# Attention and two MLPs on one core: when weights are loaded and converted beside attention, and which engine casts the activations

## The chip, the cores and the metric

The kernel runs on one core of a Trainium2 chip. The metric is the device time of one execution in microseconds (us). The runs of the kernel before took 685.08, 686.46 and 688.02 us, median 686.46. The execution that the profiler recorded took 685.12 us, of which the trace covers a span of 683.3 us; the remaining 1.8 us lie before the first and after the last recorded instruction. Differences of about half a per cent, some 3.4 us, are the smallest that can be told from no change here.

## What is computed

The reference, cut to what matters:

```python
def attention(q, k, v, n_global=8, n_local=96):      # batch 2, heads 8, seq 768, head_dim 64, fp32
    scores = q @ k.T / 8 - slope[h] * dist            # dist from |i-j|, or n_local for global columns
    keep = (j < n_global) | (0 <= i - j < n_local)
    a = softmax(where(keep, scores, -1e9))
    return a @ v

x = attention(...)            # laid out as 1536 tokens x 512
h = x @ w_in                  # 512 x 2048
g = max(h, 0) + log1p(exp(-abs(h)))
x = g @ w_out                 # 2048 x 512
h = x @ w_in2
out = (h * clip(h + 3, 0, 6) / 6) @ w_out2
```

The weights arrive as 8-byte floats. The kernel reads them as pairs of 32-bit words and makes two fp32 parts of each number, a high and a low one. Activations are split in the same way. Each product of the MLPs is then three matmuls: low by high, high by low, high by high.

## The kernel before, in words

**Tiles.** A chunk is 128 of the 2048 hidden columns of a layer; there are 16 per layer. One chunk's `w_in` is a unit, and its `w_out` another, each 512 KB in HBM and 128x512 numbers in SBUF. The class `Layers` keeps six slots for finished chunks beside attention (`FIRST_SLOTS`) and gets five more (`MORE_SLOTS`) when attention's memory is given back (`grow`).

**The order of units.** `self.order` (lines 68 to 70) puts first the `w_in` units of chunks 0 to 5 (units 0 to 5 here), then the `w_out` units of chunks 0 to 5 (units 6 to 11), then chunk by chunk. `unit_load` (L102 to L107) asks SP for the 512 KB into a tile `raw`. `unit_convert` (L109 to L134) makes the two parts in seven steps on three engines: absolute value on ScalarE (L121), clamp on GpSimd (L124), shift (L125) and two merges with the raw words (L128, L129) on VectorE, the cast of the high part (`cast`, L98 on GpSimd while `in_first` holds, L100 on ScalarE afterwards) and the subtraction that gives the low part on VectorE (L134). Each step needs the one before it. The low part is what TensorE waits for.

**Raw buffers.** There are two `raw` and two `wa` tiles beside attention (pool `wr0`), and two more of each after `grow`. `weight_step` (L136 to L147) keeps loads ahead of the conversions by as many units as there are raw buffers.

**The first part of the program.** It mixes attention with the first phase of layer 0, which runs over chunks 0 to 5 in pairs. Attention is cut into 24 quads (four heads of 128 rows); a quad has a score step `s` (TensorE scores L445, VectorE bias and row minimum L451, ScalarE exponential L456, row sums L341 and L342 on VectorE, normalisation of `pm` on GpSimd L344), two transpose steps `t` (L477, copied by ScalarE L479) and a value step `v` (L495; the result is cast at L502 and split at L503). Five quads are started ahead of the first matmul of the MLP, in the loop with `LEAD_UNITS`, the number of units that `weight_step` converts after each of the five.

`run` then goes over halves of items. An item is 256 tokens with one pair of chunks; its first half (`first_h`, tile `hf`) makes `h`, then `split_g` makes `g` and its two parts (`ghf`, `glf`), and its second half (`first_o`, tile `accf`) multiplies by `w_out`. The halves come as h0, h1, h2, o0, h3, o1, h4, o2, h5, o3 and so on. Each half carries one score step and one value step ahead of its 24 matmuls, and transposes after the sixth and the eighteenth. After the matmuls of a half it calls `weight_step` with the next number of `HALF_UNITS` (L313 and L314). So before, units 0 to 3 are asked for in the lead, unit 4 after h0, unit 5 after h1, units 6 and 7 after h2, and one more after each of o0, h3, o1 and h4. h2 needs units 4 and 5, o0 needs 6 and 7, o1 needs 8 and 9, o2 needs 10 and 11.

**What sets the order.** A scheduler places the instructions of each engine. Instructions given to `keep_in_program_order` keep their order among themselves: TensorE's in this part, and L121. Everything else goes where the scheduler's own estimate puts it, after what it depends on. On the chip each engine then takes its list strictly in that order, so that one instruction that waits holds all behind it.

**Between the parts.** After 20 halves all quads are done; `run` closes attention's pools and calls `grow`. The rest of the first phase (h11, o9 and so on to o17) runs without attention, together with the conversion of units 12 to 21. Then follow the phases of whole items (`item`), 512 tokens and one chunk each.

Of the kernel before, what the change touches and what calls it, by code (L numbers as in the profile page):

```python
# [10 lines left out]
I32 = mybir.dt.int32  # L11
# [5 lines left out]
P = 128  # L17
# [8 lines left out]
CW = 512  # L26
# [4 lines left out]
LEAD_UNITS = (0, 1, 1, 1, 1)  # L31
HALF_UNITS = (1, 1, 2, 1, 1, 1, 1)
# [16 lines left out]
class Layers:  # L49
# [6 lines left out]
    def __init__(self, ctx, tc, weights, xsh, xsl, out):  # L56
        self.ctx, self.tc, self.nc = ctx, tc, tc.nc
        self.weights, self.xsh, self.xsl, self.out = weights, xsh, xsl, out
        self.pool("mp", 2)
        self.pool("tp", 5)  # L60
        self.pool("pp", 1)
        self.part = [self.pp.tile([P, 4, GB], F32, name=f"part{g}") for g in range(T // GB)]
        self.three = self.pp.tile([P, 1], F32, name="three")
        self.nc.vector.memset(self.three, 3.0)
        self.W, self.raws, self.slot = {}, {}, {}
        self.done, self.loaded = 0, 0
        first = range(PHASES[0][0])
        self.order = [(j, u) for u in range(2) for j in first]
        self.order += [(j, u) for j in range(len(first), 2 * NCH) for u in range(2)]
        self.free, self.h_tags, self.acc_tags, self.wr = [], [], [], []  # L70
        self.n_h, self.halves, self.in_first = 0, 0, True
        self.grow(0, FIRST_SLOTS, 2, 2)
# [22 lines left out]
    def cast(self, out, in_):  # L95

        if self.in_first:
            self.nc.gpsimd.tensor_scalar(out=out, in0=in_, scalar1=1.0, scalar2=0.0, op0=ALU.mult, op1=ALU.add)  # L98
        else:
            self.nc.scalar.copy(out, in_)  # L100

    def unit_load(self, x):  # L102
        j, u = self.order[x]
        layer, f = divmod(j, NCH)
        raw = self.wr[x % len(self.wr)].tile([P, CW, 2], I32, tag="raw", name=f"raw{j}_{u}")
# [30 lines left out]
    def weight_step(self, m):  # L136
        total = 4 * NCH
        for _ in range(m):
# [3 lines left out]
            while self.loaded <= min(x + 2 * len(self.wr) - 1, total - 1):  # L142
                self.unit_load(self.loaded)
                self.loaded += 1
# [3 lines left out]
    def split_g(self, layer, hf, n):  # L148
# [6 lines left out]
        if layer == 0:  # L155
# [3 lines left out]
            if self.in_first:  # L159
# [10 lines left out]
        self.cast(gh, t3)  # L170
# [114 lines left out]
    def run(self, att=None, spare_step=lambda: None):  # L285
# [20 lines left out]
        for i in range(n):  # L306
            if not grown and (att is None or att.done()):
                if att:
                    att.close()
                self.grow(1, MORE_SLOTS, 2, 2)  # L310
# [36 lines left out]
def fast_path(tc, ident, nf, q, k, qt, kt, v, weights, out, flag):  # L347


    with ExitStack() as ctx, ExitStack() as actx:  # L350
        nc = tc.nc
        xsh, xsl = x_tiles(ctx, tc)
        layers = Layers(ctx, tc, weights, xsh, xsl, out)
        tp = layers.tp
        ap2 = actx.enter_context(tc.tile_pool(name="ap2", bufs=2))
# [410 lines left out]
```

## Time and profile before

| | |
|---|---|
| runs, us | 685.08, 686.46, 688.02 |
| profiled execution, us | 685.12 (span 683.3) |
| TensorE busy | 634.4 us, 93% of the span |
| VectorE busy | 437.8 us, 64% |
| ScalarE busy | 357.2 us, 52% |
| GpSimd busy | 166.4 us, 24% |
| mean granted TensorE clock | 0.972 of full speed |
| HBM traffic | 53 MB, 77 GB/s over the span |

PE is TensorE's matmul stream and PEld its weight loads, DVE is VectorE, ACT is ScalarE, POOL is GpSimd, SP the engine that issues all DMAs. Busy shares of TensorE also count time at half clock, so the share alone does not tell the work that is done. The page cuts the span into 40 slices of 17.1 us; a digit is the busy share in tenths. Views of the trace give, for a wait, the engine and line that ended it ("<-").

### The profile page before, as it was taken

Reading aid. Unit: us, or ns where it says so; the run is one execution under the profiler, and the core shown is the slowest. Engines: PE = TensorE matmul, PEld = TensorE weight load, DVE = VectorE, ACT = ScalarE, POOL = GpSimd, SP = SyncE. Lnnn points to the kernel's source line nnn. Section 1 sums busy time; section 2 is a strip of 40 time slices with the busy share of each in tenths; the row PEclk is TensorE's granted clock in tenths of the full one; section 3 lists DMA queues with packets and bytes.
Section 4 is the critical chain, followed back from the end, with each engine's and each line's share of the span. In section 5 each row is a group of like instructions: output and inputs, shape, how many; then the busy total and the mean of one; then the engine's idle time right before and its main releaser. Section 6 shows DMA issues by size and latency. Waiting matters only on the chain.

```text
span 683.3 us, 9612 instructions
## 1 busy us (share of the span) xinstructions
PE 634.4 (93%) x3481; PEld 522.1 (76%) x3481; DVE 437.8 (64%) x894; ACT 357.2 (52%) x749; POOL 166.4 (24%) x237
## 2 busy tenths in 40 slices
PE   8764876999997999999999999999999999999996
PEld 4553766888996988787888888888888788888884
DVE  6868345555399999999998999322752424324243
ACT  6945434776553477677677765233667222222221
POOL 4884433433255442234320021000100000000000
PEclk9988888999999999999999999999999999999998
DMA  7433323121023224142320123100265000001011
GB/s 231 143 113 116 109 66 116 39 67 55 33 93 124 94 92 147 70 154 93 123 94 31 62 64 121 63 0 1 78 197 157 1 1 0 1 0 62 0 63 66
DMA packets 24936, 53.66 MB, mean 79 GB/s; under 512 B 2480, under 2 KB 8880, under 8 KB 24880
## 3 DMA queue, kind: packets, MB, share of 16 engines
q1 hardware_dynamic: 24880, 52.96, 23.9%
q8 instruction: 29, 0.48, 0.3%
q14 instruction: 27, 0.22, 0.1%
HBM read 49.81 MB, written 3.15 MB: 77 GB/s over the span
## 4 chain that ended last, share of the span: by engine, by line
PE 65%; DVE 21%; ACT 5%; POOL 3%; issue 3%; DMA 1%; POOLq 0%; DVEq 0%; SPq 0%; ACTq 0%
PE acc L179 27%; PE h L179 26%; PE hf L179 4%; DVE wa L128 4%; PE accf L179 3%; DVE w L134 3%; DVE wa L129 3%; ACT pm L456 2%; POOL pm L344 2%; PE ptp L477 2%; PE s L445 2%; DVE wa L125 2%; PE px L495 1%; DVE pm L451 1%; DVE t2f L164 1%
## 5 line engine op out<-in xcount | busy, mean ns | idle before, releaser
L179 PE MATMUL h<-xsh,w 128*128 128x512 f32 x624 | 170.5, 396 | 1.9 <-DVE t3f L165 1.6
L179 PEld LDWEIGHTS h<-xsh,w 128*128 128x128 f32 x624 | 116.7, 188 | 30.6 <-DVE t3f L165 1.8
L179 PE MATMUL acc<-w,gh 128*128 128x512 f32 x384 | 120.6, 395 | 0.0
L124 POOL TENSOR_SCALAR wa<-wa 128x512 f32<-128x512 f32 x64 | 66.4, 1041 | 219.5 <-ACT wa L121 218.0
L169 DVE SCALAR_TENSOR_TENSOR t<-t,h 128x512 f32<-128x512 f32 x48 | 32.9, 686 | 98.2 <-ACT t L168 98.1
L168 ACT ACTIVATE t<-h,three 128x512 f32<-128x512 f32 x48 | 33.0, 687 | 107.2 <-PE h L179 107.0
L179 PE MATMUL h<-xsl,w 128*128 128x512 f32 x312 | 86.7, 395 | 0.0
L179 PE MATMUL accf<-ghf,w 128*128 128x256 f32 x288 | 66.8, 312 | 20.5 <-DVE w L134 20.4
L179 PEld LDWEIGHTS acc<-w,gh 128*128 128x128 f32 x384 | 72.0, 188 | 17.5
L171 DVE TENSOR_TENSOR gl<-t,gh 128x512 fp32r<-128x512 f32 x78 | 55.4, 710 | 46.3 <-ACT gh L100 46.1
L179 PE MATMUL acc<-gh,w 128*128 128x512 f32 x240 | 78.2, 396 | 1.3 <-DVE part L264 1.3
L100 ACT CAST gh<-t 128x512 fp32r<-128x512 f32 x78 | 48.3, 619 | 58.2 <-PE acc L179 25.6
L179 PE MATMUL acc<-w,gl 128*128 128x512 f32 x192 | 76.1, 396 | 0.1
L179 PEld LDWEIGHTS accf<-ghf,w 128*128 128x128 f32 x288 | 52.5, 211 | 23.2 <-DVE w L134 21.7
L179 PEld LDWEIGHTS h<-xsl,w 128*128 128x128 f32 x312 | 58.5, 188 | 14.0
L344 POOL TENSOR_SCALAR pm<-pm,rs 128x256 f32<-128x256 f32 (+1 forms) x96 | 52.5, 565 | 46.9 <-DVE rs L342 35.1
L134 DVE TENSOR_TENSOR w<-wa,w 128x512 fp32r<-128x512 f32 x64 | 46.5, 730 | 16.2 <-POOL w L98 8.9
L179 PEld LDWEIGHTS acc<-gh,w 128*128 128x128 f32 x240 | 45.1, 188 | 12.9 <-ACT t L157 1.7
L121 ACT ACTIVATE wa<-raw 128x512 f32<-128x512 f32 x64 | 42.5, 673 | 22.8 <-DVE w L134 14.4
L456 ACT ACTIVATE pm<-pm,nm 128x256 f32<-128x256 f32 (+1 forms) x96 | 46.2, 484 | 14.8 <-DVE nm L451 14.7
L179 PE MATMUL hf<-xsh,w 128*128 128x256 f32 x288 | 45.7, 290 | 7.9 <-DVE w L134 7.9
L451 DVE CUSTOM_DVE_ANT_0 pm<-s,bias 128x256 f32<-128x256 f32 (+1 forms) x96 | 33.4, 397 | 28.9 <-PE s L445 27.2
(90 smaller groups left out, 1008.3 us busy)
## 6 DMA issues: line engine op xcount, KB each, us to landing
raw<-in_w1i SPq DMA_DIRECT2D x16, 512.0 KB, 3.3
raw<-in_w1o SPq DMA_DIRECT2D x16, 512.0 KB, 3.3
raw<-in_w2i SPq DMA_DIRECT2D x16, 512.0 KB, 3.2
raw<-in_w2o SPq DMA_DIRECT2D x16, 512.0 KB, 3.3
V<-in_v SPq DMA_DIRECT2D x12, 256.0 KB, 2.9
chk<-in_q SPq DMA_DIRECT2D x12, 256.0 KB, 3.4
chk<-in_k SPq DMA_DIRECT2D x12, 256.0 KB, 2.8
out_x<-part SPq DMA_DIRECT2D x12, 256.0 KB, 2.1
```

What stands on the lines that cost most here:

```text
L100: self.nc.scalar.copy(out, in_)
L121: first = nc.scalar.activation(a, raw.bitcast(F32)[:, :, 1], AF.Abs)
L124: nc.gpsimd.tensor_scalar(out=a, in0=a, scalar1=W_HI, scalar2=W_LO, op0=ALU.min, op1=ALU.max)
L128: nc.vector.scalar_tensor_tensor(out=ai, in0=hi, scalar=-2 ** 30, in1=ai, op0=ALU.bitwise_and, op1=ALU.bitwise_or)
L134: nc.vector.tensor_tensor(out=wl, in0=a, in1=r32(wh), op=ALU.subtract)
L168: nc.scalar.activation(t1, hf, AF.Relu, bias=self.three[:, 0:1])
L169: nc.vector.scalar_tensor_tensor(out=t3, in0=t1, scalar=6.0, in1=hf, op0=ALU.min, op1=ALU.mult)
L171: nc.vector.tensor_tensor(out=gl, in0=t3, in1=r32(gh), op=ALU.subtract)
L179: return self.nc.tensor.matmul(out, lhsT=a, rhs=b, start=start and z == 0, stop=stop and z == len(seq) - 1, **kw)
L344: nc.gpsimd.tensor_scalar(out=t, in0=t, scalar1=rs[:, j:j + 1], scalar2=0.0, op0=ALU.mult, op1=ALU.add)
L451: nc.vector.tensor_tensor_reduce(out=pmz, in0=ps[z % 2][:, z // 2, 0:nsl, :].rearrange("p s t -> p (s t)"), in1=bias[:, 4 * e + z, mo:mo + ...
L456: nc.scalar.activation(pmz, pmz, AF.Exp, bias=nm[:, z:z + 1], scale=-1.0, accum_out=sm[:, z:z + 1])
```

## The change

Three things change. More units are asked for in the lead (6 instead of 4) and the rest in the first five halves: unit 6 and 7 after h0, 8 after h1, 9 after h2, 10 after o0, 11 after h3. Two more raw buffers (pool `ap_r`) live in attention's memory, used by units 0 to 11 alone; while attention runs, loads go up to four units ahead as long as they stay within units 0 to 11. And the choice between GpSimd and ScalarE follows `beside`, which ends with attention, instead of `in_first`, which ends with the first phase; the cast of the activations (`ghf`) is always on ScalarE.

```diff
-LEAD_UNITS = (0, 1, 1, 1, 1)
-HALF_UNITS = (1, 1, 2, 1, 1, 1, 1)
+LEAD_UNITS = (0, 1, 1, 2, 2)
+HALF_UNITS = (2, 1, 1, 1, 1)
+RAW_BUFS = 4
...
     def cast(self, out, in_):
-        if self.in_first:
+        if self.beside:
             self.nc.gpsimd.tensor_scalar(out=out, in0=in_, scalar1=1.0, scalar2=0.0, op0=ALU.mult, op1=ALU.add)
         else:
             self.nc.scalar.copy(out, in_)
     def unit_load(self, x):
...
-        raw = self.wr[x % len(self.wr)].tile([P, CW, 2], I32, tag="raw", name=f"raw{j}_{u}")
+        pools = self.wr + self.more_raw if x < 2 * PHASES[0][0] else self.wr
+        raw = pools[x % len(pools)].tile([P, CW, 2], I32, tag="raw", name=f"raw{j}_{u}")
...
     def weight_step(self, m):
...
-            while self.loaded <= min(x + 2 * len(self.wr) - 1, total - 1):
+            ahead = 2 * len(self.wr + self.more_raw)
+            if self.beside:
+                ahead = min(ahead, max(2 * PHASES[0][0] - x, 2))
+            while self.loaded <= min(x + ahead - 1, total - 1):
...
     def split_g(self, layer, hf, n):
...
-            if self.in_first:
+            if self.beside:
                 nc.gpsimd.tensor_scalar(out=t2, in0=t1, scalar1=1.0, scalar2=1.0, op0=ALU.mult, op1=ALU.add)
             else:
                 nc.scalar.add(t2, t1, 1.0)
...
-        self.cast(gh, t3)
+        nc.scalar.copy(gh, t3)
...
     def run(self, att=None, spare_step=lambda: None):
...
                 if att:
                     att.close()
+                    self.beside, self.more_raw = False, []
                 self.grow(1, MORE_SLOTS, 2, 2)
...
 def fast_path(...):
...
         layers = Layers(ctx, tc, weights, xsh, xsl, out)
+        layers.beside = True
         tp = layers.tp
+        layers.more_raw = [actx.enter_context(tc.tile_pool(name="ap_r", bufs=RAW_BUFS - 2))]
```

How the scheduler's lists move shows at three places. In them `wa_u` is the working tile of a unit (u is 0 for `w_in`, 1 for `w_out`), `w_c` a finished part of chunk c, `t2f`, `t3f` and `glf` the tiles of `split_g`, `pm`, `nm`, `rs` those of a score step, and the last number is only an identity.

**VectorE, around the matmuls of o0 and h3.** Before, the chunk-3 `w_out` unit (unit 9, on which o1 waits) stands here, behind the split of h3:

```order
L125 TENSOR_SCALAR wa_1_1025<-wa_1_1025 128x512
L341 TENSOR_SCALAR rs_1070<-sm_1057 128x4
L128 SCALAR_TENSOR_TENSOR wa_1_1025<-raw_1_941,wa_1_1025 128x512
L342 RECIPROCAL rs_1070<-rs_1070 128x4
L503 TENSOR_TENSOR xsl_81<-px_976,xsh_78 128x4x128
L129 SCALAR_TENSOR_TENSOR wa_1_1025<-raw_1_941,wa_1_1025 128x512
L164 SCALAR_TENSOR_TENSOR t2f_1037<-t2f_1037,t1f_1035 128x512
L165 SCALAR_TENSOR_TENSOR t3f_1036<-hf_4_951,t3f_1036 128x512
L134 TENSOR_TENSOR w_3_537<-wa_1_1025,w_3_536 128x512
```

Now, units 8 and 9 (chunks 2 and 3) follow unit 7 (chunk 1) directly, one item earlier, right after the split of h2:

```order
L170 SCALAR_TENSOR_TENSOR t3f_875<-hf_3_791,t3f_875 128x512
L127 TENSOR_SCALAR wa_1_769<-wa_1_769 128x512
L171 TENSOR_TENSOR t3f_875<-t3f_875,t2f_876 128x512
L136 TENSOR_TENSOR w_1_414<-wa_1_666,w_1_413 128x512
L130 SCALAR_TENSOR_TENSOR wa_1_769<-raw_1_567,wa_1_769 128x512
L131 SCALAR_TENSOR_TENSOR wa_1_769<-raw_1_567,wa_1_769 128x512
L127 TENSOR_SCALAR wa_1_864<-wa_1_864 128x512
L130 SCALAR_TENSOR_TENSOR wa_1_864<-raw_1_654,wa_1_864 128x512
L136 TENSOR_TENSOR w_2_476<-wa_1_769,w_2_475 128x512
L131 SCALAR_TENSOR_TENSOR wa_1_864<-raw_1_654,wa_1_864 128x512
L136 TENSOR_TENSOR w_3_490<-wa_1_864,w_3_489 128x512
L176 TENSOR_TENSOR glf_873<-t3f_875,ghf_872 128x512
```

The last step of unit 9 moved from behind the split of h3 (tile `hf_4`) to behind that of h2 (tile `hf_3`), with no score step between it and unit 8. The last step of unit 7, on which o0 waits, still stands behind the split of h2 as it did before.

**VectorE, the first item after attention.** Before, the low part `glf` of h11 (tile `hf_12`) stands behind two units (12 and 13) and two steps of a third:

```order
L165 SCALAR_TENSOR_TENSOR t3f_2251<-hf_12_2205,t3f_2251 128x512
L134 TENSOR_TENSOR w_6_2237<-wa_0_2240,w_6_2236 128x512
L166 TENSOR_TENSOR t3f_2251<-t3f_2251,t2f_2252 128x512
L125 TENSOR_SCALAR wa_1_2290<-wa_1_2290 128x512
L128 SCALAR_TENSOR_TENSOR wa_1_2290<-raw_1_2230,wa_1_2290 128x512
L129 SCALAR_TENSOR_TENSOR wa_1_2290<-raw_1_2230,wa_1_2290 128x512
L125 TENSOR_SCALAR wa_0_2329<-wa_0_2329 128x512
L128 SCALAR_TENSOR_TENSOR wa_0_2329<-raw_0_2232,wa_0_2329 128x512
L171 TENSOR_TENSOR glf_2249<-t3f_2251,ghf_2248 128x512
```

Now it stands behind the first unit alone, and the next item's split follows at once:

```order
L170 SCALAR_TENSOR_TENSOR t3f_2255<-hf_12_2209,t3f_2255 128x512
L136 TENSOR_TENSOR w_6_2241<-wa_0_2244,w_6_2240 128x512
L171 TENSOR_TENSOR t3f_2255<-t3f_2255,t2f_2256 128x512
L176 TENSOR_TENSOR glf_2253<-t3f_2255,ghf_2252 128x512
L169 SCALAR_TENSOR_TENSOR t2f_2345<-t2f_2345,t1f_2343 128x512
```

Five steps of weights that stood ahead of this `glf` moved behind it.

**SP, in the lead.** Before, two loads of raw weights stand ahead of the queries of attention's block 2:

```order
L374 DMA kT<-in_kt 128x4x128
L375 DMA V_247<-in_v 128x512
L106 DMA raw_0_335<-in_w1i 128x1024
L106 DMA raw_0_337<-in_w1i 128x1024
L373 DMA qT_246<-in_qt 128x512
```

Now there are four:

```order
L382 DMA kT<-in_kt 128x4x128
L383 DMA V_250<-in_v 128x512
L108 DMA raw_0_338<-in_w1i 128x1024
L108 DMA raw_0_340<-in_w1i 128x1024
L108 DMA raw_0_342<-in_w1i 128x1024
L108 DMA raw_0_344<-in_w1i 128x1024
L381 DMA qT_249<-in_qt 128x512
```

Two loads of 512 KB each moved ahead of this block's queries.

## Rows read from the trace of the kernel before

**Rows 1.** The page: TensorE's busy tenths and its granted clock in 40 slices.
```profile
PE   8764876999997999999999999999999999999996
...
PEclk9988888999999999999999999999999999999998
```

**Rows 2.** Busy time by stretch: length; PE, PEld, DVE, ACT, POOL; clock, DMA share, GB/s.
```profile
60.00:80.00 20.00, 10.57 (x76) 9.45 (x73) 11.31 (x29) 7.06 (x23) 7.10 (x11) 0.74 0.29 92
80.00:100.00 20.00, 14.12 (x118) 13.06 (x117) 10.08 (x34) 9.22 (x27) 8.74 (x14) 0.83 0.32 100
```

**Rows 3.** Waits of PE between 30 and 130 us: total, times, longest.
```profile
PE accf L179 <- DVE w L134: 20.4, 4, 5.9
PE hf L179 <- DVE w L134: 7.9, 3, 5.2
```

**Rows 4.** Timeline of all engines between 74 and 100 us, unit 9 on its way.
```profile
81.91 0.68 ACT L121 ACTIVATE wa<-raw 128x512 f32<-128x512 f32 x1
...
86.36 2.47 POOL L344 TENSOR_SCALAR pm<-pm,rs 128x128 f32<-128x128 f32 x4 [0.86 <-ACT t3f L163]
...
89.45 0.69 DVE L134 TENSOR_TENSOR w<-wa,w 128x512 fp32r<-128x512 f32 x1 [0.88 <-POOL w L98]
```

**Rows 5.** Timeline of PE, first matmuls of halves and of what waited: start, length, idle before.
```profile
83.70 0.38 PE L179 MATMUL accf<-ghf,w 128*128 128x256 f32 x1
...
90.20 0.58 PE L179 MATMUL accf<-ghf,w 128*128 128x256 f32 x1 [5.88 <-DVE w L134]
...
97.73 0.74 PE L179 MATMUL hf<-xsh,w 128*128 128x256 f32 x4
...
103.90 0.38 PE L179 MATMUL accf<-ghf,w 128*128 128x256 f32 x1
...
109.64 0.58 PE L179 MATMUL accf<-ghf,w 128*128 128x256 f32 x1 [5.12 <-DVE w L134]
...
117.12 0.74 PE L179 MATMUL hf<-xsh,w 128*128 128x256 f32 x4
...
135.37 0.39 PE L179 MATMUL accf<-ghf,w 128*128 128x256 f32 x1
...
142.01 0.74 PE L179 MATMUL hf<-xsh,w 128*128 128x256 f32 x4
```

**Rows 6.** Waits of PE between 190 and 245 us, and one stretch there, columns as above.
```profile
PE accf L179 <- DVE glf L171: 3.0, 1, 3.0
PE h L179 <- DVE t3f L165: 1.6, 1, 1.6
...
208.00:212.00 4.00, 3.83 (x20) 3.83 (x21) 4.00 (x8) 0.72 (x2) 2.23 (x3) 0.59 0.27 87
```

**Rows 7.** Groups by form on DVE, 188 to 236 us and then 236 to 340: count | busy us, mean ns.
```profile
L128 DVE SCALAR_TENSOR_TENSOR wa<-raw,wa 128x512 int32<-128x512 int32 x10 | 9.0, 898 | 0.1
L171 DVE TENSOR_TENSOR glf<-t3f,ghf 128x512 fp32r<-128x512 f32 x6 | 6.0, 1003 | 0.8 <-POOL ghf L98 0.8
...
L128 DVE SCALAR_TENSOR_TENSOR wa<-raw,wa 128x512 int32<-128x512 int32 x22 | 16.2, 736 | 0.0
L171 DVE TENSOR_TENSOR gl<-t,gh 128x512 fp32r<-128x512 f32 x16 | 11.8, 737 | 0.0
```

**Rows 8.** Timeline of all engines from 42 us, the split of h0 and unit 3.
```profile
42.13 0.69 DVE L164 SCALAR_TENSOR_TENSOR t2f<-t2f,t1f 128x512 f32<-128x512 f32 x1 [0.33 <-ACT t3f L163]
...
44.34 0.69 DVE L134 TENSOR_TENSOR w<-wa,w 128x512 fp32r<-128x512 f32 x1
...
55.95 0.74 PE L179 MATMUL hf<-xsh,w 128*128 128x256 f32 x4 [1.99 <-DVE w L134]
```

**Rows 9.** Group by form on ACT, 240 to 340 us.
```profile
L100 ACT CAST gh<-t 128x512 fp32r<-128x512 f32 x16 | 9.9, 619 | 4.9 <-DVE t L166 3.7 <-PE h L179 1.2
```

**Rows 10.** Timeline of SP in the lead, and a row of the page's DMA issues.
```profile
7.71 5.50 SPq L373 DMA_DIRECT2D qT<-in_qt  x2
...
raw<-in_w1i SPq DMA_DIRECT2D x16, 512.0 KB, 3.3
```

More of the change, by code (lines that the diff above doesn't have):

```diff
@@ L69, in __init__ @@
         self.order += [(j, u) for j in range(len(first), 2 * NCH) for u in range(2)]
-        self.free, self.h_tags, self.acc_tags, self.wr = [], [], [], []
-        self.n_h, self.halves, self.in_first = 0, 0, True
+        self.free, self.h_tags, self.acc_tags, self.wr, self.more_raw = [], [], [], [], []
+        self.n_h, self.halves, self.in_first, self.beside = 0, 0, True, False
         self.grow(0, FIRST_SLOTS, 2, 2)
```

## The prediction

> **What bounds the kernel now.** I read the page's slices first, to see where TensorE is not full. From the fifteenth slice on, some 240 us, its digit is 9 in all slices but the last: that stretch is bound by matmuls, the change leaves it alone, and what is won earlier is won at the end. Ahead of it there are digits of 8 to 4 in the first seven slices, up to 120 us, with clock digits of 8 in five of them, and a 7 in the thirteenth [rows 1]. The busy time by stretch sizes the first place: between 60 and 100 us TensorE is busy 10.6 and 14.1 of 20 us at mean clocks of 0.74 and 0.83 [rows 2]. No other engine is full there: VectorE has 11.3 and 10.1, ScalarE 7.1 and 9.2, GpSimd 7.1 and 8.7 [rows 2]. So this is not lack of capacity but a chain whose steps come late. The waits say which: between 30 and 130 us TensorE waits seven times, 28.3 us in all, for the last step of a weight unit on VectorE, L134 [rows 3].
>
> The timeline of unit 9 shows why it is late. Its first step is taken at 81.91, after the matmuls of h3, when o1, which needs it, is only one half away. Then GpSimd's 2.47 us of normalisation stand in front of its cast, and the last step comes at 89.45 [rows 4]. o1 has begun at 83.70, does three matmuls, and continues at 90.20 after 5.88 us idle [rows 5]. TensorE's list is strict, so the score steps behind these matmuls wait too, and with them all of VectorE's and ScalarE's attention work.
>
> A second, smaller place lies after attention. Between 190 and 245 us TensorE waits 3.0 us for `glf` and 1.6 us for L165, and between 208 and 212 its clock is at 0.59 [rows 6].
>
> **The change, part by part.** *Units 8 to 11, o1 and o2.* From the start of o1 to h4 it is 97.73 - 83.70 = 14.03 us, from o2 to h5 117.12 - 103.90 = 13.22; a second half without a weight wait, o4, takes 142.01 - 135.37 = 6.64 [rows 5]. The excess is 7.4 and 6.6 us, 14.0 together; it holds the two waits (5.88 and 5.12) and the matmuls behind each at the lower clock (0.58 us for the one at 90.20, 0.38 for the one at 83.70). In VectorE's new list units 8 and 9 follow unit 7 without a score step between. Unit 7 gates o0's second piece, so units 8 and 9 have the matmuls of o0 and all of h3 to finish; their remaining seven steps, at the 0.74 to 0.90 us of a merge [rows 7], are 5 to 6 us, against the rest of o0 and all of h3, close to two halves of 6.64. Units 10 and 11 are asked for two halves earlier as well. I count all 14.0 as won. Bounds: 6.6, if o1's wait stays and only o2's goes; 14.0, since no more than the excess can be won here.
>
> *Units 3 to 7, h1 to o0.* Here the lists hardly moved. Unit 3's last step stood behind two steps of h0's split, which waited for ScalarE (42.13 against 44.34 [rows 8]); now it goes ahead of that split, but behind the row sums and two steps of unit 4. Counting four such steps in place of six at 0.3 to 0.7 us gives about 1.1 us. Unit 5 is asked for in the lead, not after h1; h2's wait of 1.99 [rows 8] should go. That is 3.1 us. o0's two waits I leave as they are: unit 7 still ends behind the split of h2. They are what remains of 20.4 when o1's and o2's are taken off, 9.4 us [rows 3, 5]. Bounds: 0, as VectorE has less idle time to absorb two more units; above, 3.1 and half of o0's 9.4, 7.8.
>
> *After attention.* The casts of ten weight units (12 to 21) and of seven items and these items' additions leave GpSimd: 24 operations. VectorE's two-input steps cost more while GpSimd is active: L128 takes 898 ns and L171 1003 in 188 to 236 us, but 736 and 737 in 236 to 340 us, where GpSimd has the clamp alone [rows 7]. On these two groups that is 10 x 0.16 + 6 x 0.27 = 3.2 us given back, and `glf` of the first item moves ahead of five weight steps. TensorE's loss there is 3.0 + 1.6 us of waits and 4 x (1 - 0.59) = 1.6 us of clock [rows 6], 6.2. Bounds: 0, because VectorE is full (4.00 of 4.00 [rows 6]) and another step may be late instead; 6.2. I take 4.5, nearer the upper end, since from 240 to 340 us, with this very split of engines, TensorE's digits are 9 [rows 1]. ScalarE takes the 24 operations at 0.62 us [rows 9], 14.9 us of some 55, in a stretch where it has 0.72 of 4 us [rows 6] at the point of the stall: covered.
> The Trainium skill ("SBUF — State Buffer", section on who interferes with whom) says that GpSimd and a VectorE instruction with two SBUF inputs share one port as an exclusive lock, and that ScalarE never waits on it. The longer steps agree in kind. If each of the 24 operations blocked VectorE for its whole length the term would be at its bound of 6.2, and the sum 1.7 us better.
>
> *Four raw loads in the lead.* The queries of block 2 are issued behind four loads instead of two; SP starts on them at 7.71, and one load takes 3.3 us to land [rows 10]. Lower bound 0 (the second of these two issues waits until 13.2 anyway, 7.71 + 5.50), upper 2 x 3.3 = 6.6 if two loads delay them singly. I take 0.7, near the lower end, because VectorE is busy with the previous quad when these scores come. The raw loads themselves cost nothing else: buffers come free by the same L129 steps, two units sooner.
> The Trainium skill ("DMA: Bandwidth & Descriptors", section on queues, rings and completion order) says that each DMA engine takes one queue's descriptors in ring order: a rule against this part of the change. By it the whole landing time of the extra bytes falls on those queries, and the sum would be up to 5.9 us worse. No row before shows two loads more in front.
>
> *The cast of `ghf` on ScalarE beside attention* costs 0.62 us per item on an engine that is busy 7 to 9 of 20 us [rows 2], and takes as much from GpSimd; `glf` is needed two halves later. Nothing, either way; if ScalarE filled up, the transposes' copies would wait next.
>
> **Sum.** 14.0 + 3.1 + 4.5 - 0.7 = 20.9 us. The profiled execution goes from 685.12 to 664.2; the median of the runs lies 1.34 above it, so I predict 686.46 - 20.9 = 665.6 us.
>
> **The rivals.** *VectorE's queue moves the wait on.* Six units in the lead and two after h0 make VectorE the bound from 40 us on, unit 9 leaves it after o1's first three matmuls, and o1 keeps its wait. For it: VectorE is nearly full in that stretch once the idle time is gone. Against: 8.7 of 20 us idle at 60 to 80 us [rows 2]. Then 6.6 + 3.1 + 4.5 - 0.7 = 13.5, 673.0 us.
>
> *ScalarE becomes the bound after attention.* Its in-order list mixes casts that wait for VectorE with the exponentials and logarithms of the next items, so the stall of 6.2 us stays: 14.0 + 3.1 - 0.7 = 16.4, 670.1 us. It decides when a split waits for ScalarE longer than for VectorE.
>
> *Slower: SP's queue.* Raw loads wait for free buffers at SP's head, and queries and keys stand behind them. If in each of eight blocks TensorE's scores wait 3.3 us for a DMA [rows 10], that is 26.4 us, more than the 20.9 won: 692.0. It decides from 2.6 us per block. Against: no wait of 30 to 130 us names a DMA [rows 3].
>
> *The waits stay where they are*, because the chip's timing and the scheduler's differ so that both lists end in the same places: gain under 3 us, 684 to 687.
>
> **How the numbers follow.** The forecast 0.67, VectorE's queue 0.13, ScalarE 0.10, the slower case 0.04, no change 0.06. Half a per cent, 3.4 us, is about what the measurement can tell, so faster has 0.90, same 0.06, slower 0.04. With every term at its best the time is 686.46 - (14.0 + 7.8 + 6.2) = 658.5. Without the gain after attention it is 670.1, with o1's wait left 673.0, with both 686.46 - (6.6 + 3.1 - 0.7) = 677.5. I give 657 to 677, which leaves out the last two rivals and the corner of the first two together.
>
> **What would show it.** Right: waits of TensorE for L134 between 30 and 130 us fall from 28.3 to 10 to 14 us, those that remain are o0's, o1 and o2 take 6 to 7 us each, h5 starts near 100 us instead of 117.12, clock 1.00 from there on; the 3.0 us for `glf` after attention is gone; VectorE's L128 after attention is near 740 ns. Wrong: o1 still waits over 3 us for L134; TensorE waits for a DMA; or the stretch after attention shows waits that end on ScalarE.

## The result, and the profile after

The changed kernel takes 660.38 us (median of four runs, 660.01 to 660.76) against 685.77 us for the kernel before in the same series: a ratio of 0.9625, 95% interval 0.9599 to 0.9651, faster by 25.4 us. The forecast was 665.6 us, a gain of 20.9. The executions that the profiler recorded, 685.12 and 660.44 us, differ by 24.7, and it is on these that the terms can be checked.

The page of the changed kernel, TensorE's busy tenths and granted clock in 40 slices, as in [rows 1]:

```profile
PE   7975899999999999999999999999999999999995
...
PEclk9888799999999999999999999999999999999999
```

TensorE's digit is 9 from the sixth slice on, some 82 us, in all but the last slice. Before, it was so from the eighth slice on, some 120 us, but for the 7 of the thirteenth, which is gone. The busy time of the two stretches of [rows 2], same columns (length; PE, PEld, DVE, ACT, POOL; clock, DMA share, GB/s):

```profile
60.00:80.00 20.00, 12.78 (x102) 11.50 (x98) 17.33 (x43) 9.68 (x27) 11.74 (x16) 0.83 0.41 130
80.00:100.00 20.00, 19.67 (x191) 17.35 (x190) 14.73 (x52) 15.80 (x47) 11.30 (x20) 1.00 0.30 87
```

TensorE went from 14.1 to 19.7 of 20 us in the second. In the first VectorE went from 11.3 to 17.3: it is nearly the bound there now. The waits of TensorE between 30 and 130 us, as in [rows 3]:

```profile
PE accf L184 <- DVE w L136: 7.2, 2, 5.6
PE hf L184 <- DVE w L136: 6.8, 3, 3.3
```

28.3 us have become 14.0. They are five, and TensorE's timeline has them one by one (start, length, what, idle before):

```profile
34.94 0.74 PE L184 MATMUL hf<-xsh,w 128*128 128x256 f32 x4 [0.92 <-DVE w L136]
44.47 0.74 PE L184 MATMUL hf<-xsh,w 128*128 128x256 f32 x4 [3.28 <-DVE w L136]
54.93 0.75 PE L184 MATMUL hf<-xsh,w 128*128 128x256 f32 x4 [2.62 <-DVE w L136]
62.29 0.38 PE L184 MATMUL accf<-ghf,w 128*128 128x256 f32 x1 [1.59 <-DVE w L136]
68.54 0.58 PE L184 MATMUL accf<-ghf,w 128*128 128x256 f32 x1 [5.62 <-DVE w L136]
```

They stand at the second pieces of h0, h1 and h2 (a piece is the half's twelve matmuls of one chunk), at the start of o0 and, within o0, at the first matmul of its second chunk; none is at o1 or o2. The same timeline at the starts of [rows 5] (o1, h4, o2, h5, o4, h7):

```profile
81.72 0.39 PE L184 MATMUL accf<-ghf,w 128*128 128x256 f32 x1
...
87.29 0.75 PE L184 MATMUL hf<-xsh,w 128*128 128x256 f32 x4
...
93.29 0.39 PE L184 MATMUL accf<-ghf,w 128*128 128x256 f32 x1
...
98.95 0.74 PE L184 MATMUL hf<-xsh,w 128*128 128x256 f32 x4
...
117.61 0.39 PE L184 MATMUL accf<-ghf,w 128*128 128x256 f32 x1
...
124.20 0.74 PE L184 MATMUL hf<-xsh,w 128*128 128x256 f32 x4
```

o1 takes 5.57 us (14.03 before) and o2 5.66 (13.22). h5 starts at 98.95 instead of 117.12: 18.17 us of the gain lie ahead of it. Later starts in the same timeline place the rest: the o half that begins at 182.10 us before begins at 164.22 now (17.88 apart), the last run of matmuls at 670.68 and 645.92 (24.76). So -0.3 us lie between, and 24.76 - 17.88 = 6.9 us after that o half, which is the last one beside attention. From 150 to 300 us TensorE's only wait of 0.3 us or more is one of 0.3; those for `glf` and for the split [rows 6] are gone. VectorE's groups by form from 170 to 216 us, the stretch that answers to the first of [rows 7]:

```profile
L130 DVE SCALAR_TENSOR_TENSOR wa<-raw,wa 128x512 int32<-128x512 int32 x10 | 7.5, 755 | 0.1
...
L176 DVE TENSOR_TENSOR glf<-t3f,ghf 128x512 fp32r<-128x512 f32 x6 | 4.1, 684 | 1.7 <-ACT ghf L175 1.7
```

755 ns and 684 ns, where the same steps took 898 and 1003. The one place that got worse is the lead; waits of TensorE from 0 to 30 us:

```profile
PE s L453 <- DMA kT<-in_kt: 2.3, 2, 2.1
PE s L453 <- DMA qT<-in_qt: 2.0, 1, 2.0
```

h0 starts at 31.89 us instead of 30.79.

### The profile page after: what moved, and what is told of

Its sections match the earlier page's. It is cut to its first block, busy times and chain, and to the rows that moved or that the text cites. A ratio compares the mean times of both kernels' runs of the same rounds, so it can differ in the third digit from the quotient of the medians.

```text
span 658.6 us, 9592 instructions
## 1 busy us (share of the span) xinstructions
PE 627.6 (95%) x3480; PEld 517.3 (79%) x3481; DVE 430.7 (65%) x894; ACT 376.0 (57%) x786; POOL 146.8 (22%) x200
## 4 chain that ended last, share of the span: by engine, by line
PE 71%; DVE 17%; ACT 4%; POOL 3%; DMA 2%; issue 2%; SPq 0%; DVEq 0%; ACTq 0%; POOLq 0%
PE h L184 26%; PE acc L184 26%; PE hf L184 7%; PE accf L184 6%; PE s L453 2%; PE ptp L485 2%; DVE wa L131 2%; DVE w L136 2%; DVE wa L130 2%; ACT pm L464 2%; POOL pm L350 2%; PE px L503 2%; DVE t L170 1%; DVE t L169 1%; DVE gl L176 1%
## 5 line engine op out<-in xcount | busy, mean ns | idle before, releaser
L126 POOL TENSOR_SCALAR wa<-wa 128x512 f32<-128x512 f32 x64 | 73.5, 1153 | 255.5 <-ACT wa L123 253.8
L176 DVE TENSOR_TENSOR gl<-t,gh 128x512 fp32r<-128x512 f32 x78 | 54.6, 699 | 43.8 <-ACT gh L175 43.4
L184 PEld LDWEIGHTS h<-xsl,w 128*128 128x128 f32 x312 | 58.7, 188 | 14.1
L184 PE MATMUL accf<-ghf,w 128*128 128x256 f32 x288 | 60.5, 294 | 7.2 <-DVE w L136 7.2
L184 PEld LDWEIGHTS accf<-ghf,w 128*128 128x128 f32 x288 | 47.9, 193 | 9.2 <-DVE w L136 7.7
L123 ACT ACTIVATE wa<-raw 128x512 f32<-128x512 f32 x64 | 42.9, 673 | 20.9 <-DVE w L136 18.4
L136 DVE TENSOR_TENSOR w<-wa,w 128x512 fp32r<-128x512 f32 x64 | 44.8, 701 | 12.4 <-ACT w L101 8.7
L184 PE MATMUL acc<-gl,w 128*128 128x512 f32 x120 | 47.5, 396 | 0.0
```

The source lines that it names most:

```text
L123: first = nc.scalar.activation(a, raw.bitcast(F32)[:, :, 1], AF.Abs)
L126: nc.gpsimd.tensor_scalar(out=a, in0=a, scalar1=W_HI, scalar2=W_LO, op0=ALU.min, op1=ALU.max)
L136: nc.vector.tensor_tensor(out=wl, in0=a, in1=r32(wh), op=ALU.subtract)
L176: nc.vector.tensor_tensor(out=gl, in0=t3, in1=r32(gh), op=ALU.subtract)
L184: return self.nc.tensor.matmul(out, lhsT=a, rhs=b, start=start and z == 0, stop=stop and z == len(seq) - 1, **kw)
```

## The experiments

### Taking the change apart

Three theories stood open: the gain is a sum of a table's part ahead of h5 and a part of the engine choice after attention, with nothing from the raw buffers; or the parts need each other; or one part alone does both. Four kernels tell them apart.

**The tables alone**, on the kernel before:

```diff
-LEAD_UNITS = (0, 1, 1, 1, 1)
-HALF_UNITS = (1, 1, 2, 1, 1, 1, 1)
+LEAD_UNITS = (0, 1, 1, 2, 2)
+HALF_UNITS = (2, 1, 1, 1, 1)
```

> The kernel before with the two tables of the changed one alone: six units in the lead, two after h0, then one; two raw buffers, casts and additions as before. Theory (three parts that add up): the tables win what the trace shows up to h5, some 18 us, and nothing after attention: 667 to 669 us, o1 and o2 without a wait for the weights, h5 near 99 us, the 3 us wait for glf after attention still there. Rival (parts need each other): with two raw buffers, or with the cast of ghf on GpSimd, units 8 to 11 come late again, o1 keeps a wait of over 3 us, 673 us or more. Second rival (the order clears the stall after attention too): 660 to 663.

Measured: 666.71 us (ratio 0.9703, 0.9687 to 0.9719), span 666.1 against 683.3 before, h5 at 99.58 us, no wait of o1 or o2 for weights. This is the theory, if 0.3 us under its range: 17.2 us of span, nearly all ahead of h5. What is left after attention is the old stall; its wait of TensorE between 180 and 200 us, and VectorE's group by form between 170 and 216 us:

```profile
PE accf L179 <- DVE glf L171: 3.0, 1, 3.0
```

```profile
L128 DVE SCALAR_TENSOR_TENSOR wa<-raw,wa 128x512 int32<-128x512 int32 x10 | 9.0, 895 | 0.1
```

**The engine choice alone**, on the kernel before:

```diff
+        layers.beside = True
...
-        if self.in_first:
+        if self.beside:
...
-        self.cast(gh, t3)
+        nc.scalar.copy(gh, t3)
...
+                    self.beside = False
```

> The kernel before with the engine choice of the changed one alone: the cast of the activations on ScalarE always, the weights' casts and the additions on ScalarE from the end of attention on; old tables, two raw buffers. Theory: this wins the stall after attention and nothing ahead of it: 679 to 681 us, o1 and o2 still wait 5 to 6 us each, h5 near 117 us, no wait of over 1 us for glf after attention. Rival (it is the tables that clear the stall, by leaving VectorE less behind when attention ends): 684 to 687, the wait for glf still near 3 us. Second rival (freeing GpSimd of seven casts beside attention brings units 8 to 11 earlier): under 675, h5 before 112 us.

Measured: 678.56 us (0.9887, 0.9863 to 0.9911), 0.4 us under the theory's range, span 676.4, so 6.9 us of span. h5 is at 117.49 us, as before, and TensorE's largest wait from 0 to 130 us is still this one:

```profile
PE accf L184 <- DVE w L136: 19.4, 4, 5.8
```

After attention TensorE has no wait for `glf` at all. The two parts add up: 17.2 + 6.9 = 24.1 us of span, and the changed kernel has 683.3 - 658.6 = 24.7. By the medians they are 20.0 and 8.1 us, together 28.1 against 25.4; that difference of 2.7 us is about as large as the intervals of the three runs together allow.

**Two raw buffers**, the changed kernel without the added pool:

```diff
-        layers.more_raw = [actx.enter_context(tc.tile_pool(name="ap_r", bufs=RAW_BUFS - 2))]
```

> The changed kernel with two raw buffers beside attention instead of four, all else as it is. Theory: the two more buffers are worth nothing and cost the queries' wait in the lead: 659 to 661 us, scores wait under 1.5 us for queries and keys in the first 30 us, h0 starts near 30.8 us instead of 31.89. Rival (two raw buffers can't feed units two halves ahead): loads come late, waits of ScalarE for raw in the early part, 664 us or more.

Measured: 660.84 us (0.9613, 0.9592 to 0.9634): the buffers are worth nothing in time, as the theory had it. But its second half is wrong: h0 starts at 32.29 us, not earlier. In the lead the profile puts a wait of 2.6 us of TensorE's scores down to a step of VectorE in place of the DMA, and the tables alone, also with two raw buffers, wait for a DMA of the keys in the first 32 us:

```profile
PE s L445 <- DMA kT<-in_kt: 2.4, 1, 2.4
```

The raw loads do not explain this wait: SP has asked for the keys of the first three blocks by 5.43 us and asks for the first raw weights at 6.69, in the same order as before, where the same scores waited 1.0 us. Why the keys land later isn't settled.

The rival's sign did appear, though not its time. Waits of ScalarE and TensorE from 30 to 130 us with two raw buffers:

```profile
ACT wa L123 <- DMA raw<-in_w1o: 4.9, 3, 1.9
ACT wa L123 <- DMA raw<-in_w1i: 1.2, 1, 1.2
PE ptp L484 <- ACT pT L486: 8.3, 7, 2.6
PE hf L184 <- DVE w L136: 7.1, 4, 4.8
PE accf L184 <- DVE w L136: 0.8, 1, 0.8
```

ScalarE stands 6.1 us before raw weights, and the copies of the transposes behind them in its list come late: TensorE waits 8.3 us for these (1.9 with four buffers) and only 7.9 for weights (14.0). The sum is about the same. So a total of waits with one name is no measure of the time by itself.

**The old engine choice in the changed kernel** (tables and raw buffers):

```diff
-        if self.beside:
+        if self.in_first:
...
-        nc.scalar.copy(gh, t3)
+        self.cast(gh, t3)
```

> The changed kernel with the engine choice of the one before (casts of weights and activations and the additions on GpSimd through all of the first phase): new tables, four raw buffers. Theory: as the tables alone, 667 to 669 us, the stall after attention there with some 3 us for glf and VectorE's second merge step near 0.9 us there. Rival (the stall after attention is gone without the casts): 660 to 663. Second rival (raw buffers matter): over 2 us faster than the tables alone.

Measured: 667.35 us (0.9724, 0.9706 to 0.9741), with a wait of 3.3 us for `glf`: the tables' gain, with or without buffers.

### What the engine choice does after attention

Two ways were left by which 26 operations (twelve casts of weights, of which the forecast counted ten, seven of activations, seven additions) cost time on GpSimd: VectorE's steps get longer beside them, or the results are late because they stand in GpSimd's list.

**Casts of weights and additions back on GpSimd** until the first phase ends, the activations' cast on ScalarE (the same edit at both places, in `cast` and in `split_g`):

```diff
-        if self.beside:
+        if self.in_first:
```

> The changed kernel, but the weights' casts and the items' additions stay on GpSimd until the first phase ends, not until attention ends; the cast of the activations stays on ScalarE. Theory (GpSimd's operations lengthen VectorE's two-input steps in a stretch where VectorE is full): some two thirds of the operations are back, so about two thirds of the 6.5 us between the changed kernel and the tables alone are lost, 663 to 666 us, L130 after attention between 0.80 and 0.90 us. Rival (glf was late only because its cast stood in GpSimd's list behind five weight steps): the cast on ScalarE is enough, 660 to 662 us, no wait of over 1 us of TensorE after attention.

Measured: 665.61 us (0.9695, 0.9664 to 0.9725). 5.2 us are lost with 19 of the 26 operations back, so the activations' cast alone is not what cleared the stall. It clears part of it: TensorE waits 0.8 us for `glf` and 1.8 us for `t3f` after attention, where the old engine choice has 3.3 and 1.5. VectorE's first merge between 160 and 240 us:

```profile
L130 DVE SCALAR_TENSOR_TENSOR wa<-raw,wa 128x512 int32<-128x512 int32 x14 | 11.3, 808 | 0.2
```

808 ns lie between the changed kernel's 755 to 761 and the 898 before, at the lower edge of what was expected.

**The activations' cast on GpSimd beside attention only**:

```diff
-        nc.scalar.copy(gh, t3)
+        self.cast(gh, t3)
```

> The changed kernel, but the cast of the activations goes to GpSimd while attention runs and to ScalarE after it. Theory: the half that was costed at nothing is worth nothing, 659.5 to 661.5 us. Rival (the cast on ScalarE is what frees GpSimd for the weights beside attention): h5 starts 2 us later or more, 662.5 us or more.

Measured: 660.83 us (0.9628, 0.9593 to 0.9663), h5 at 98.92 us. Nothing, as costed.

**Useless copies beside each operation that had left GpSimd**:

```diff
+    def extra(self, in_):
+        if self.in_first and self.scratch is not None:
+            self.nc.gpsimd.tensor_scalar(out=self.scratch, in0=in_, scalar1=1.0, scalar2=0.0, op0=ALU.mult, op1=ALU.add)
...
             self.nc.scalar.copy(out, in_)
+            self.extra(in_)
...
                 nc.scalar.add(t2, t1, 1.0)
+                self.extra(t1)
...
         nc.scalar.copy(gh, t3)
+        self.extra(t3)
```

> The changed kernel with one more GpSimd operation of 128x512 beside each cast and addition that left GpSimd after attention (26 in the first phase); each copies the same tile to a scratch tile that nobody reads, and ScalarE keeps the work itself. Theory (VectorE's steps are longer while GpSimd is active): L130 after attention rises from 0.76 us towards 0.90, VectorE has no idle time to take it, and much of the stall comes back: 664 to 668 us. Rival (it was the way through GpSimd's list that made the steps late, not the length of VectorE's): 660 to 662 us, whatever L130 does.

Measured: 672.58 us (0.9785, 0.975 to 0.982), beyond both. The run was meant to load the port and did more: the copies read tiles that VectorE and ScalarE make and reuse. Waits between 185 and 245 us, and the stretch 220 to 240:

```profile
POOL scratch L109 <- DVE wa L139: 12.0, 3, 5.8
```

```profile
220.00:240.00 20.00, 18.31 (x101) 15.53 (x101) 14.57 (x24) 16.82 (x30) 12.65 (x14) 1.00 0.25 80
```

GpSimd stands 12 us before copies that wait for VectorE, the next units' clamps stand behind them, ScalarE waits for tiles that a copy still reads, and VectorE is idle 5.4 of 20 us. Its first merge is not longer, as the theory had expected, but 734 ns from 180 to 245 us. So list order can cost time too, but this run doesn't separate the two.

**Copies that nobody waits for**, two for each of the twelve units, from the raw integers:

```diff
+        if self.in_first and self.scratch is not None:
+            for _ in range(2):
+                nc.gpsimd.tensor_scalar(
+                    out=self.scratch, in0=raw.bitcast(F32)[:, :, 1], scalar1=1.0, scalar2=0.0, op0=ALU.mult, op1=ALU.add
+                )
```

> The changed kernel with two more GpSimd operations of 128x512 for each of the twelve weight units converted after attention in the first phase: they copy the unit's raw integers, which lie ready, to a scratch tile that nobody reads, so they wait for no other engine's step and hold no tile that a later step writes. Theory (GpSimd's activity alone lengthens VectorE's two-input steps and VectorE has no room): L136-type and merge steps between 180 and 245 us rise from 0.69 to 0.76 us to 0.80 to 0.90, VectorE stays full, waits of TensorE for t3f and glf come back, 663 to 667 us. Rival (what cost the time was the way of the casts through GpSimd's list, which waits for VectorE): steps may get longer, but 660 to 661.5 us and no wait of over 1 us.

Measured: 665.77 us (0.9695, 0.9681 to 0.971): 5.4 us lost by activity of GpSimd on which no result depends. The busy time from 180 to 245 us, this kernel and then the changed one:

```profile
180.00:245.00 65.00, 62.62 (x405) 56.18 (x404) 62.48 (x97) 51.00 (x89) 29.92 (x30) 1.00 0.31 101
```

```profile
180.00:245.00 65.00, 65.00 (x416) 58.74 (x416) 62.94 (x106) 53.19 (x94) 15.79 (x16) 1.00 0.34 114
```

VectorE is as busy in both, but got 97 steps done instead of 106: nine steps at 62.94/106 = 0.59 us, 5.3 us (a rough size, since the two recorded executions differ by 4.1 us of span). It is idle 2.5 of the 65 us here and 2.1 in the changed kernel, and in the trace no engine ever waits for one of the copies (they themselves wait, 9.3 us for raw weights to land and once 4.4 us for VectorE): so steps that came late in a list are at most a small part of this. Its groups by form there (L137 is the first merge, L176 the split's step behind the logarithm):

```profile
L137 DVE SCALAR_TENSOR_TENSOR wa<-raw,wa 128x512 int32<-128x512 int32 x14 | 11.2, 799 | 0.0
...
L176 DVE SCALAR_TENSOR_TENSOR t2f<-t2f,t1f 128x512 f32<-128x512 f32 x6 | 5.4, 900 | 1.5 <-ACT t3f L175 1.5
```

799 and 900 ns, in the changed kernel 755 and 730. That GpSimd's activity by itself lengthens VectorE's steps, and that this costs time where VectorE is full, is shown. As the theory said, a wait of TensorE for `t3f` is back (2.3 us); one for `glf` is not. How much of the 6.9 us was this and how much the order of the lists was not measured apart.

### Trying for more

VectorE is busy 43.6 of 50 us between 30 and 80 us, and that is where the remaining 14.0 us of waits stand.

**Weights' casts on ScalarE beside attention too:**

```diff
-        self.cast(wh, a)
+        self.nc.scalar.copy(wh, a)
```

> The changed kernel with the weights' casts on ScalarE beside attention too (the additions stay on GpSimd there). Theory: between 30 and 80 us VectorE is the bound (43.6 of 50 us busy) and its two-input steps are 0.7 to 1.1 us beside GpSimd; twelve casts less on GpSimd and no wait behind the normalisation give back 2 to 5 us of the 14.0 us for which TensorE still waits for weights: 655.5 to 658.5 us. Rival (ScalarE's list is in order and the casts wait in it for VectorE, so the exponentials and the copies of the transposes come late): 660 to 665 us, with more waits of TensorE for pT.

Measured: 661.45 us (0.9617, 0.958 to 0.9654), no gain. GpSimd's busy time from 30 to 80 us fell from 34.2 to 25.6 us and VectorE's from 43.6 to 42.3, but the lead grew: h0 starts at 34.81 us, and o0 at 62.38, where it was (62.29).

**The same from the fourth unit on:**

```diff
-        self.cast(wh, a)
+        (self.nc.scalar.copy if x > 2 else self.cast)(wh, a)
```

> The changed kernel with the weights' casts on ScalarE from the fourth unit on, beside attention too, and on GpSimd for the first three units. Theory: with all casts on ScalarE the lead took 2.9 us longer (h0 at 34.81 instead of 31.89), but h0 to o0 2.8 us less (27.6 instead of 30.4); keeping the lead's first casts on GpSimd takes the second without the first, 657 to 659 us, h0 before 32.5 us. Rival (the two are one: what the lead lost was the same VectorE work, only done earlier): 660 to 662.5 us, o0 near 62 us as in both.

Measured: 662.52 us (0.9637, 0.9619 to 0.9655). h0 is at 34.74 us again, though the first three casts were GpSimd's. What delays the lead is not a cast at all: in these two traces the first step of the first unit is taken at 20.26 and 20.34 us, in the changed kernel at 17.10, so the lead is 3.2 us behind before anything has been cast. The stretch from 10 to 15 us, with all casts on ScalarE and then in the changed kernel:

```profile
10.00:15.00 5.00, 5.00 (x17) 2.78 (x18) 1.92 (x10) 0.87 (x6) 4.75 (x14) 0.50 1.04 409
10.00:15.00 5.00, 4.84 (x37) 2.86 (x35) 2.58 (x12) 3.51 (x16) 4.75 (x14) 1.00 1.00 401
```

After a wait of 2.6 us for keys (2.1 in the changed kernel) TensorE runs there at a clock of 0.50, the lower of its two levels, and does 17 matmuls instead of 37; with the casts from the fourth unit on it is the same (0.50). The recorded executions took 663.4 and 665.88 us, where the medians are 661.45 and 662.52. So these runs do not show that the longer lead is a price of the edit; why the clock fell in both stays open. From h0 to o0 it is 27.6 and 30.2 us in the two and 30.4 in the changed kernel, from h0 to h5 66.3, 67.9 and 67.1: of the 2.8 us that the first seemed to win little is left.

**The first three units asked for sooner**, each by one step of the lead:

```diff
-LEAD_UNITS = (0, 1, 1, 2, 2)
+LEAD_UNITS = (1, 1, 1, 1, 2)
```

> The changed kernel with the same six units in the lead asked for earlier, (1, 1, 1, 1, 2) in place of (0, 1, 1, 2, 2). Theory: VectorE has 8 of its first 20 us idle and is the bound from 40 us on, so a first unit taken some 5 us sooner moves the weights of h1 to o0 forward; 1 to 4 us of the 14.0 us of waits go, 656.5 to 659.5 us. Rival (the scores of the lead come later because GpSimd and VectorE do units in front of them, and what the halves gain the lead loses): h0 after 33 us, 660 to 663 us.

Measured: 655.61 us (0.9547, 0.9531 to 0.9563), better than the changed kernel by some 5 us. The lead is about as long as the longest of the other runs with six units there (h0 at 32.30, the two with casts on ScalarE left aside). TensorE's timeline, the waits for weights that are left:

```profile
49.10 1.22 PE L184 MATMUL hf<-xsh,w 128*128 128x256 f32 x4 [3.43 <-DVE w L136]
54.54 1.22 PE L184 MATMUL hf<-xsh,w 128*128 128x256 f32 x4 [1.66 <-DVE w L136]
62.93 0.39 PE L184 MATMUL accf<-ghf,w 128*128 128x256 f32 x1 [1.97 <-DVE w L136]
```

They are at both pieces of h2 and at the second chunk of o0, where 5.62 us have become 1.97; those at h0, h1 and the start of o0 are gone. h5 starts at 92.67 us, 6.3 earlier.

**Seven units in the lead**, one after each half:

```diff
-LEAD_UNITS = (0, 1, 1, 2, 2)
-HALF_UNITS = (2, 1, 1, 1, 1)
+LEAD_UNITS = (1, 1, 1, 2, 2)
+HALF_UNITS = (1, 1, 1, 1, 1)
```

> The changed kernel with seven units in the lead, (1, 1, 1, 2, 2), and one after each half, in place of (0, 1, 1, 2, 2) and two after h0. Against the run with (1, 1, 1, 1, 2), 655.61 us, units 4 and 6 are asked for one step earlier; its trace still has 7.1 us of waits of TensorE for weights, at h1, h2 and o0. Theory (each step that a unit is asked for sooner moves its end sooner): 651 to 654.5 us. Rival (VectorE, busy 9.7 of 10 us from 20 to 30 us there and 45.4 of 50 from 30 to 80, has no more room, and what units gain the scores lose): 655 to 659 us.

Measured: 655.76 us (0.9544, 0.9516 to 0.9573), the same as with six: the rival's time. VectorE is busy 9.74 of 10 us from 20 to 30 us and 45.0 of 50 from 30 to 80. But that it is VectorE that stops the gain is not shown. A second limit fits as well: a unit's first step writes one of two `wa` tiles, and the unit two before must be through with that tile. The first steps of units 4 and 6, which were asked for one step sooner here, with six and then with seven units in the lead:

```profile
37.49 0.69 ACT L123 ACTIVATE wa<-raw 128x512 f32<-128x512 f32 x1
...
49.16 0.68 ACT L123 ACTIVATE wa<-raw 128x512 f32<-128x512 f32 x1
...
37.63 0.71 ACT L123 ACTIVATE wa<-raw 128x512 f32<-128x512 f32 x1
...
49.37 0.66 ACT L123 ACTIVATE wa<-raw 128x512 f32<-128x512 f32 x1
```

They begin no sooner, and 0.1 to 0.4 us after units 2 and 4 have ended (37.27 and 49.24 us in the second run). In the changed kernel too, each of units 2 to 9 begins 0.03 to 0.64 us after the end of the unit two before it. A third `wa` tile was not tried, so which of the two limits holds stays open.

## Why the prediction was right, and where its terms were off

The direction and the two main mechanisms held: the single-part runs found the gain ahead of h5 and the gain after attention where they had been forecast, and each without the other. The sum was 3.8 us short on the profiled execution: 20.9 against 24.7. Measured, its terms are 16.0 + 3.2 + 6.9 - 1.1, with the -0.3 us between h5 and the end of attention that had no term.

*Units 8 to 11, o1 and o2*: forecast 14.0, measured (14.03 - 5.57) + (13.22 - 5.66) = 16.0. The mechanism is the one forecast: with the tables alone both halves run without a wait for weights. The mis-sized term is the excess, and with it the upper bound of 14.0 that was said to be all there is. The yardstick was o4 at 6.64 us. But halves are not alike; what lies between the start of o1 or o4 and the next half differs (the changed kernel's timeline, the score step behind o1's matmuls and then the one behind o4's):

```profile
85.62 0.71 PE L453 MATMUL s<-kT,qT 64*128 64x128 f32 x8
...
122.11 1.13 PE L453 MATMUL s<-kT,qT 64*128 64x256 f32 x8
```

Behind o1 stand the scores of the first block of a batch, which are half as wide, behind o4 those of the full width (o2 likewise carries half-width transposes and values of such a block, and o4 also waits 0.41 us for a copy). The right yardstick was a half with the same quad in it.

*Units 3 to 7, h1 to o0*: forecast 3.1, measured from h0's start to h3's 47.33 before and 44.16 after, 3.2. That the size agrees is luck, for the places do not. h1's second wait fell from 5.2 to 3.28 (forecast 1.1 us of gain, got 1.9). h2's wait, which "should go", is 2.62 instead of 1.99. And o0's start, "left as it is", fell from 4.41 to 1.59, while its second chunk's wait rose from 5.02 to 5.62. The step that failed was to expect unit 5's end where its request went. Its way in the changed kernel, a normalisation on GpSimd, then the unit's first step, its clamp and its last step:

```profile
43.27 3.73 POOL L350 TENSOR_SCALAR pm<-pm,rs 128x256 f32<-128x256 f32 x4
...
44.45 0.68 ACT L123 ACTIVATE wa<-raw 128x512 f32<-128x512 f32 x1 [1.26 <-DVE w L136]
...
47.67 1.11 POOL L126 TENSOR_SCALAR wa<-wa 128x512 f32<-128x512 f32 x1
...
54.19 0.68 DVE L136 TENSOR_TENSOR w<-wa,w 128x512 fp32r<-128x512 f32 x1
```

It begins when unit 3 has left the `wa` tile (44.42), its clamp stands behind 3.73 us of normalisation on GpSimd, and its last step behind a score step on VectorE, which is busy 9.2 of 10 us from 50 to 60 us. So this unit, asked for earlier, was paced by the unit two before it, by GpSimd's list and by VectorE's, and not by its request. Only the last of these is the first rival, on a smaller scale and one half earlier than it was put.

*After attention*: forecast 4.5 of at most 6.2, measured 6.9. The stall is gone to the last wait. The bound itself was a little small: it counted two waits and one stretch of clock, and left out a wait of 1.3 us for `part` (L264 before), of which 0.3 are left. The count of operations was 26, not 24, since units 22 and 23 are converted in the first phase too.
Of the two groups that carried the estimate, L130 (L128 before) came to 755 ns and L176 to 684, where 740 was forecast. Together these two gave back 10 x 0.14 + 6 x 0.32 = 3.3 us, as forecast (3.2). Steps that were not counted got shorter too, the subtraction of the low part (L134 before, L136 now) from 808 to 699 ns and two steps of the split (L164 and L166, now L169 and L171) from 889 and 884 to 725 and 683. The useless copies show the same mechanism from the other side: 24 of them cost 5.4 us, 0.22 us each.
The Trainium skill ("SBUF — State Buffer", section on who interferes with whom) has an exclusive lock between GpSimd and a VectorE step with two SBUF inputs, and the trace agrees in kind, since VectorE's steps are longer. By the prediction's sentence the sum would have been 22.6, nearer to the 24.7. But 0.22 us per copy is far below the 0.65 us of the shortest of these copies: on average they did not hold VectorE for their whole length.

*The lead*: forecast -0.7, measured -1.1, and its step is only half seen. The price was to be four raw loads in front of the queries. The wait for a DMA that was listed among the signs of a wrong forecast did appear, here alone: 2.0 us for these queries, and 2.1 us for keys that are asked for ahead of all raw loads. But with two raw loads in front h0 was no earlier (32.29), and the old engine choice in the changed kernel has waits of 1.7 and 2.1 us for keys and queries and h0 at 30.78, as early as before (30.79). What goes with the start of h0 is the clock granted in the lead: from 15 to 25 us it is 1.00 there and before, 0.83 in the changed kernel. With four units in the lead h0 is at 30.57 and 30.79 us. With the six of the change, the runs with casts on ScalarE left aside, it is at 30.78 and 31.45 in the two runs without a stretch of 5 us under 1.00 up to 40 us, and between 31.35 and 32.36 in the six with one. The forecast had no term for this clock. A raw load in the lead also took 6.2 us to land before (median of the two issued up to 20 us), not the 3.3 of the whole trace.
The Trainium skill ("DMA: Bandwidth & Descriptors", section on queues, rings and completion order) would have made it up to 5.9 us worse. A wait of 2 us for queries behind the loads agrees in kind; the whole landing time was not lost, since before these scores came only at 15.01 us, 7.3 us after the queries were asked for.

*The cast of `ghf`*: forecast nothing, measured 0.4 us apart with intervals that overlap.

*The rivals.* o1 kept no wait, so VectorE's queue did not decide there. ScalarE did not become the bound after attention: it is busy 53.2 of 65 us from 180 to 245 us, and no wait of TensorE there is for it. In the blocks after the lead no score waits for a DMA, so SP's queue was not slower.

## What to carry to other kernels

A wait for a late result is first a question of when it was asked for: two lines of a table were worth 20 us of median, more than twice the engine choice, and moving the first requests of the lead once more was worth another 5. Keep on until an earlier request no longer makes the work begin earlier (here with the seventh unit in the lead), and then look at what the work waits for instead: an engine that is nearly full (here VectorE), or a buffer that the work two before still holds (here `wa`). When an excess is read as "this half against an undisturbed one", compare halves that carry the same side work. And when two traces differ, compare the granted clock of the same stretch before naming the edit as the cause.

## What was not expected of the hardware

Moving work from GpSimd to another engine was worth time although GpSimd was not full (busy 12.2 of 20 us before at 200 to 220 us), and part of that is the room that VectorE gets. Work on GpSimd lengthens also VectorE's one-input step, the shift and mask of the weights (L127, L134 in the kernel with the copies that nobody waits for): 443 ns on average in the changed kernel and 520 in that one, from 180 to 245 us. And an operation of GpSimd can itself be longer there: a copy of 0.62 us took 0.93 in the run with copies beside each operation:

```profile
207.51 0.62 POOL L109 TENSOR_SCALAR scratch<-t1f 128x512 f32<-128x512 f32 x1
207.52 1.15 DVE L178 SCALAR_TENSOR_TENSOR t2f<-t2f,t1f 128x512 f32<-128x512 f32 x1 [0.57 <-ACT t3f L177]
...
208.21 0.93 POOL L109 TENSOR_SCALAR scratch<-t3f 128x512 f32<-128x512 f32 x1
...
208.59 0.68 DVE L179 SCALAR_TENSOR_TENSOR t3f<-hf,t3f 128x512 f32<-128x512 f32 x1
```

The first copy and VectorE's step begin 0.01 us apart: the copy keeps its 0.62 us, and the step, 0.68 where it is undisturbed, takes 1.15. The second copy begins while that step still runs and takes 0.93, while VectorE's next step, with one of its two operands in PSUM (`hf`), stays at 0.68 beside it.
